# Attention and routed experts on one core: three of four turns of the values moved from the fifth block of a step to the first block of the next one

## The chip, the core and the metric

The kernel runs on one core of a Trainium2 chip. The metric is the device time of one execution in microseconds, taken as the median of several. A core has five engines that run side by side, each through its own queue in order: PE (matrix products; its weight loads, PEld, run beside them), DVE (VectorE), ACT (ScalarE), POOL (GpSimd) and SP (SyncE, which here issues DMAs). They meet through semaphores.

## The reference, cut to what matters

The program computes attention with rotary positions and feeds the result to a layer of routed experts. There are 8 batches of 8 heads, 576 positions, 64 features each.

```python
q_rot, k_rot = (rotate(q), rotate(k))
scores = scale * np.matmul(q_rot, k_rot.transpose(0, 1, 3, 2))
scores = scores - np.max(scores, axis=-1, keepdims=True)
attn = np.exp(scores)
attn = attn / (np.sum(attn, axis=-1, keepdims=True) + 1e-09)
attn_out = np.matmul(attn, v)                    # (8, 8, 576, 64)

x = attn_out.transpose(0, 2, 1, 3).reshape(4608, 512)
y_dense = np.maximum(x @ w1_dense, 0.0) @ w2_dense
logits = x @ w_gate                              # 8 experts
expert_idx = np.argmax(logits, axis=1)           # softmax of logits gives gate_w
y_moe[mask] = gate_w[mask, None] * (np.maximum(x[mask] @ w1[e], 0.0) @ w2[e])   # for each expert e
out = y_dense + y_moe
```

## The kernel before, in words

**Stages.** Attention takes the span from about 29 to 318 us of the profiled execution, the experts' layer the rest. Attention runs over 32 pairs of heads, four pairs to a batch. All of it is issued in program order (a manual schedule), so each engine's queue holds its instructions in the order in which the Python code calls them; no planner moves anything.

**A step and its blocks.** The main loop runs over steps i and, inside a step, over blocks t = 0 to 8. Three pairs are in the works at once. In block t of step i:

- `s1_block(i + 2, t)`, the **scores** of the pair two steps ahead, row-wise: two products on PE (lines 365 and 369, tile `s` of PSUM tag `s1`, two buffers), and DVE takes each row's maximum from them (line 371, `negm`).
- `s2_strip(i, t)`, the **logits** of the present pair, key-wise, with the maximum already folded in: a product on PE (lines 389, 390, 392; PSUM tag `s2`, two buffers), and ACT takes the exponential from it into `pm` (line 409).
- `av_part(i - 1, k)`, the product of the previous pair's exponentials with the values (line 431), from block 1 on; one part of five products in most blocks, two parts in some. After block 8 `av_scale` divides on DVE (lines 442 to 445).

In block 1, `shift_rows(i + 1)` turns the next pair's maxima on PE (line 377, `mps`, tag `s2`), splits them on ACT and DVE (lines 379 and 380, `mT`) and sends them by two DMAs into two rows of `qT` (line 382). The logits of the next step need these rows. After block 8 come the tails, `s2_tails` (lines 389, 390 and 392 again, exponentials on line 416): a use of tag `s2` for the last 64 queries of eight key blocks, and one for the ninth.

**The values.** Each pair's values are loaded in fp32 (`vf`), cast to fp16 on ACT (`cast_v`, line 273) into `v16s`, and turned: `v_turn` (lines 281 and 282) makes five 128 by 128 transposes on PE into a PSUM tile `vps` of tag `s2`, and ACT copies them into `vT`. When all four pairs of a batch are turned, `v_gate` (line 290) multiplies them by the gate's weights at the end of the batch's first step, i = 4b, and `v_part` (lines 298 and 300) puts the result beside the values, so that the attention product also gives the experts' logits. The table `v_steps` says in which step and block a cast and a turn are called; turns of this table come after the block's scores, logits and value products.

**Tag `s2`.** Logits, tails, shifts, turns and gates take the two buffers of this tag by turns. A use can begin when all readers of the use before last are through.

**Other work beside it.** POOL rotates the queries and keys of later pairs (lines 314 to 317) and issues the loads of the experts' weights (line 226); SP issues the transposing DMAs (`qT<-nat`, line 327), the copies of keys (`kx<-qT`, line 355), and the loads. From step 27 on the routing of the first six batches is computed between the blocks, on DVE, POOL, ACT and PE.

Of the kernel before, what the change touches and what calls it, by code (L numbers as in the profile page):

```python
# [25 lines left out]
def kernel(  # L26
# [40 lines left out]
    for i in range(VB):  # L67
        t = const_p.tile([P, HP, 5, 2 * VC], fp16, name=f"v16_{i}")
# [6 lines left out]
    with tc.tile_pool(name="setup", bufs=1) as setup_p:  # L75
# [37 lines left out]
        for b0, b1 in ((0, 5), (5, 9)):  # L113
            n = b1 - b0
# [242 lines left out]
    def s1_block(i, t):  # L357
        qT, kT = (x[0:KM] for x in state["qkT", i])
        if t == 0:
            state["negm", i] = ap.tile([P, 9], f32, tag="negm", bufs=3, name="negm")  # L360
        ps = pp.tile([P, 2, 512], f32, tag="s1", bufs=2, name="s1")
        for c in range(2):
            if t == 4:
                for r0, q0, k0 in ((0, AT, A0), (64, BT, B0)):
                    nc.tensor.matmul(ps[r0:r0 + 64, c, 0:CH], lhsT=qT[:, q0:q0 + 64],  # L365
                                     rhs=kT[:, k0 + c * CH:k0 + (c + 1) * CH], start=True, stop=True)
            else:
                k0 = A0 if t < 4 else B0
                nc.tensor.matmul(ps[:, c, 0:CH], lhsT=qT[:, t * P:(t + 1) * P],  # L369
                                 rhs=kT[:, k0 + c * CH:k0 + (c + 1) * CH], start=True, stop=True)  # L370
        nc.vector.tensor_reduce(state["negm", i][:, t:t + 1], ps[:, :, 0:CH], axis=AX.XY, op=AL.max, negate=True)  # L371
# [299 lines left out]
    def attention():  # L671
        for f in turn_early(0):
            f()
        stage_keys(1, nc.sync)
        for part in range(2):
            stage_load(1, 0, 2, part, (0, HP))
        split_gate()
        for i in range(1, KK):
            pad_keys(i)
        for t in range(9):  # L680
            s1_block(0, t)
        for t in range(9):
            s1_block(1, t)
            if t == 1:
                shift_rows(0)
                for part in range(2):
                    stage_load(1, 2, 4, part, ())
                nc.scalar.copy(ident_h, ident_f)
                nc.scalar.preload_act_table_set("natural_log_exp_and_others")
                cast_v(0, 0)  # L690
            if t == 2:
                early_2 = turn_early(2)
            if 3 <= t < 7:
                early_2[t - 3]()
        cast_v(0, 1)
        for i in range(3, RA):
            stage_rope(i)
        stage_transpose(3)
        gt = gate_steps(0, wg)
        rk, got0 = rank_steps(0, wg, attn_sums)  # L700
        WS = [(i, 5) for i in range(5, 22, HP)] + [(24, 5), (25, 1), (25, 6), (26, 1), (26, 6)]
        assert len(WS) == E + 2
        steps = {(27, 0): gt[0:1], (22, 0): [route_first, route_ranks, route_tokens], (27, 2): gt[1:2], (27, 4): gt[2:3]}
        AVS = (((0, 0), (0, 1), (1, 3), (3, 4), (4, 5), (5, 7), (7, 8), (8, 9), (9, 10)),
               ((0, 0), (0, 1), (1, 3), (3, 4), (4, 5), (5, 6), (6, 7), (7, 8), (8, 10)))
        loads = {}
        for b in range(2, B):
            n = (b - 2) * HP
            for at, f, *x in ((n, stage_load, b, 0, 2, 0, ()), (n + 1, stage_load, b, 0, 2, 1, ()),
                              (n + 1, stage_tails, b, 0), (n + (1 if b in (2, B - 1) else 2), stage_tails, b, 1),  # L710
                              (n + 2, stage_load, b, 2, 4, 0, ()), (n + 3, stage_load, b, 2, 4, 1, ())):
                loads.setdefault(at + (1 if b == 2 else 0), []).append((f, *x))
        V0 = (0, 2), (0, 7), (1, 3), (1, 5)
        v_steps = {}
        for b in range(1, B):
            n = b * HP
            for u, (c, r) in enumerate((((n - 3, 6), (n - 3, 8)), ((n - 2, 3), (n - 2, 5)), ((n - 1, 3), (n - 1, 5)), ((n, 2), (n, 5)))):
                if b == B - 1 and u > 1:
                    c = (n - 1, 1 + 3 * (u - 2))
                if b == 1 and u < 2:  # L720
                    c, r = ((n - 2, 1), (n - 2, 5)) if u == 0 else ((n - 2, 6), (n - 2, 8))
                v_steps.setdefault(c, []).append((cast_v, b, u))
                v_steps.setdefault(r, []).append((v_turn, b, u))
        for i in range(NP + 1):
            for t in range(9):
                if i + 2 < NP:
                    s1_block(i + 2, t)
                if i < NP:
                    s2_strip(i, t)
                if 1 <= i <= NP and t >= 1:  # L730
                    for k in range(*AVS[i % HP == 1][t]):
                        av_part(i - 1, k)
                    if t == 8:
                        av_scale(i - 1)
                if i == 0 and t in (3, 5):
                    cast_v(0, 2 + t // 5)
                if (i, t) in V0:
                    v_turn(0, V0.index((i, t)))
                if i < NP and (i, t) in v_steps:
                    for f, *x in v_steps.pop((i, t)):  # L740
                        f(*x)
                if t == 1 and i + 1 < NP:
                    shift_rows(i + 1)
                if t == 2 and i + RA < NP:
                    stage_rope(i + RA)
                if t == (0 if i > 1 else 2) and i + KA < NP:
                    stage_keys(i + KA, nc.sync)
                if t == 2 and i + LA < NP:
                    stage_transpose(i + LA)
                if t == 2:  # L750
                    for f, *x in loads.pop(i, ()):
                        f(*x)
                if (i, t) in WS:
                    n = WS.index((i, t))
                    load_w(*((w1d, moe_w1_dense), (w2d, moe_w2_dense))[n] if n < 2 else (w1e[:, n - 2], moe_w1[n - 2]))
                if t == 5:

                    if i % HP == 0 and i // HP + 1 < B:
                        stage_v(i // HP + 1)
                    if i % HP == 3 and HP < i < NP - HP or i == NP - 3:  # L760
                        x_store(i // HP - 1)
                    if i == NP - RA:
                        early_cm.__exit__(None, None, None)
                        open_late()
                        wa = late["wa"]
                        pl, mm, fin = plan_steps(0, wa, attn_sums, got0)
                        w2 = [lambda e=e: load_w(late["w2e"][:, e], moe_w2[e]) for e in range(E)]
                        steps[27, 6] = rk[0:1] + [route_parts]
                        steps[27, 5] = w2[0:2]
                        steps[27, 7] = w2[2:5]  # L770
                        steps[28, 0] = rk[1:2] + w2[5:6] + pl[0:1]
                        steps[28, 2] = gt[3:4]
                        steps[28, 3] = rk[2:3] + w2[6:8] + pl[1:2]
                        steps[28, 6] = rk[3:4]
                        steps[29, 0] = pl[2:3]
                        steps[30, 5] = pl[3:4]
                        steps[29, 3] = pl[4:6]
                        steps[29, 8] = rk[4:5]
                        steps[30, 0] = rk[5:6]
                        steps[30, 2] = mm + [fin, lambda: draw(0, 0)]  # L780
                        steps[30, 6] = [lambda: draw(0, 2)]
                if (i, t) == (NP - 2, 4):
                    logit_sum(B - 2)
                for st in steps.pop((i, t), ()):
                    st()
            if i < NP:
                s2_tails(i, 0)
            if i < NP:
                s2_tails(i, 1)
            if i in (0, 1) or i < NP and i % HP == 0:  # L790
                u0, u1 = (2 * i, 2 * i + 2) if i < 2 else (0, HP)
                for u in range(u0, u1, 2):
                    v_gate(u)
                v_part(i // HP, 0, u0, u1)
                steps.setdefault((i + 1, 0), []).append(lambda b=i // HP, u0=u0, u1=u1: v_part(b, 1, u0, u1))
            if i == NP - 1:
                draw(1, 0)
                draw(1, 2)
        assert not steps and not v_steps and not loads
        logit_sum(B - 1)  # L800
        x_store(B - 1)

# [248 lines left out]
```

## Time and profile before

| | |
|---|---|
| median of 3 runs | 466.23 us (463.81 to 466.33) |
| the profiled execution | 465.76 us |
| its span, first to last instruction | 464.0 us |
| mean granted clock of PE | 0.984 |
| busy: PE, DVE, ACT, POOL | 404.8, 320.5, 294.0, 342.3 us |
| transposes of the values (line 281) | 160, busy 14.1 us |
| copies of the turned values (line 282) | 32, busy 22.1 us, 692 ns each |
| exponentials of the logits (line 409, 512 wide) | 280, 598 ns each |
| maxima of the scores (line 371) | 288, 749 ns each |

How to read it: busy times are sums over the span, and a group's mean is the time from an instruction's start to its end; the next one on the same engine can begin a little before that. In the order of time each row gives start, length, engine, line, operation, out<-in, shapes and count, and in brackets the engine's idle time before it with what ended it.

### The profile page before, as it was taken

The page shows a single profiled execution, that of the slowest core. Times are in us where ns is not written, and L with a number is a line of the kernel's source. Part 1 is how long each engine was busy: PE and PEld are TensorE (multiplying, and loading weights), DVE is VectorE, ACT ScalarE, POOL GpSimd, SP SyncE. Part 2 cuts the span into 40 slices and gives each one's busy share as a digit, 9 for nine tenths or more (in the row PEclk, how much of TensorE's full clock was granted, in tenths as well). Part 3 has the DMA queues.
Part 4 walks back from the last instruction along what each step waited for, and adds up shares of the span by engine and source line. Part 5 has one row for each costly group of instructions (what it writes and reads, how often), then busy time and mean ns, then how long its engine had stood idle before and what let it go on. Part 6 is the DMA issues. An engine that isn't in the chain of part 4 may idle for free.

```text
span 464.0 us, 11073 instructions
## 1 busy us (share of the span) xinstructions
PE 404.8 (87%) x4108; PEld 250.0 (54%) x4108; DVE 320.5 (69%) x580; ACT 294.0 (63%) x571; POOL 342.3 (74%) x279
## 2 busy tenths in 40 slices
PE   1788898889999999999998879777999999999992
PEld 0346566666666666666666556554344544444440
DVE  7886799889999899899899899933357221111221
ACT  6588787877887987887887876653443323333320
POOL 1799999989999889999999958834464456652332
PEclk9999999999999999999999998989999999999998
DMA  6886669987867967988959999954988588996452
GB/s 177 227 172 156 119 159 243 143 198 209 178 192 195 179 192 201 167 194 209 202 151 209 157 148 220 217 95 95 207 193 163 135 202 190 199 188 147 97 146 84
DMA packets 134250, 80.65 MB, mean 174 GB/s; under 512 B 93460, under 2 KB 127764, under 8 KB 134196
## 3 DMA queue, kind: packets, MB, share of 16 engines
q1 hardware_dynamic: 119684, 55.93, 54.0%
q0 software_dynamic: 14240, 23.73, 25.2%
q8 instruction: 35, 0.57, 0.5%
q10 hardware_dynamic: 272, 0.26, 0.2%
q14 instruction: 19, 0.16, 0.1%
HBM read 52.05 MB, written 14.42 MB: 143 GB/s over the span
## 4 chain that ended last, share of the span: by engine, by line
PE 62%; DVE 11%; DMA 10%; ACT 9%; issue 3%; SPq 2%; another core or an unknown queue 1%; POOLq 0%; POOL 0%; ACTq 0%; DVEq 0%
PE s L369 10%; PE s L392 9%; PE av L431 9%; PE py L922 7%; PE py L920 7%; PE pe L905 6%; PE pd L896 6%; DVE negm L371 5%; ACT pm L409 5%; DMA qT<-mT 3%; DMA kx<-qT 2%; PE vps L281 2%; PE s L365 2%; PE s L389 2%; DMA vf<-in_v_dram 2%
## 5 line engine op out<-in xcount | busy, mean ns | idle before, releaser
L371 DVE TENSOR_REDUCE negm<-s 128x1 f32<-128x576 f32 x288 | 205.3, 749 | 20.3 <-PE s L369 19.0
L409 ACT ACTIVATE pm<-s 128x512 f16<-128x512 f32 x280 | 161.3, 598 | 42.0 <-PE s L392 36.1
L431 PEld LDWEIGHTS <-pm 128*128 128x128 f16 x1600 | 87.1, 98 | 53.8 <-issue 21.4
L392 PE MATMUL s<-qT,kx 128*128 128x64 bf16 (+1 forms) x504 | 107.0, 285 | 9.8 <-ACT pm L409 4.5
L369 PE MATMUL s<-kx,qT 126*128 126x288 bf16 x512 | 108.0, 294 | 6.3 <-DVE negm L371 4.3
L431 PE MATMUL av<-v,pm 128*128 128x82 f16 x1600 | 100.5, 201 | 1.0 <-DVE v L300 0.7
L314 POOL TENSOR_TENSOR ra<-qk,cosx 128x1152 bf16<-128x1152 f32 x30 | 78.9, 2630 | 20.1 <-DVE nat L317 10.9
L924 DVE COPY y<-py 128x512 f32<-128x512 f32 x37 | 25.2, 690 | 86.0 <-PE py L922 66.9
L925 POOL DMA_INDIRECT out_dram<-y,put_i x37 | 38.1, 1030 | 57.9 <-DVE y L924 49.2
L908 ACT ACTIVATE hn<-pe,gp 128x512 bf16<-128x512 f32 x37 | 25.4, 687 | 75.5 <-PE pe L905 35.0
L317 POOL TENSOR_TENSOR nat<-ra,rb 128x1152 bf16<-128x1152 bf16 x30 | 70.9, 2363 | 2.4
L851 POOL DMA_INDIRECT xg<-xd,take_i x37 | 35.8, 967 | 25.7 <-issue 9.4
L369 PEld LDWEIGHTS <-qT 126*128 126x128 bf16 x512 | 40.2, 99 | 20.9 <-issue 13.1
L905 PE MATMUL pe<-w1e,xs 128*128 x148 | 38.9, 385 | 4.2 <-ACT hn L908 2.5
L392 PEld LDWEIGHTS <-kx 128*128 128x128 bf16 x512 | 35.1, 97 | 13.1 <-issue 5.2
L315 POOL TENSOR_TENSOR rb<-qk,sinx 128x576 bf16<-128x576 f32 x30 | 42.2, 1406 | 0.0
L316 POOL TENSOR_TENSOR rb<-qk,sinx 128x576 bf16<-128x576 f32 x30 | 42.1, 1404 | 0.0
L896 PE MATMUL pd<-xs,w1d 128*128 128x512 bf16 (+1 forms) x160 | 38.6, 369 | 0.2 <-ACT hd L898 0.2
L922 PE MATMUL py<-w2e,he 128*128 x148 | 38.0, 379 | 0.5 <-DMA he<-hn 0.5
L920 PE MATMUL py<-w2d,hd 128*128 128x512 bf16 x148 | 38.0, 379 | 0.0
L898 ACT ACTIVATE hd<-pd 128x512 bf16<-128x512 f32 (+1 forms) x40 | 22.6, 565 | 10.1 <-PE py L922 4.8
L443 DVE TENSOR_TENSOR xn<-av,rz 128x640 bf16<-128x640 f32 x32 | 26.4, 825 | 1.1
(178 smaller groups left out, 428.0 us busy)
## 6 DMA issues: line engine op xcount, KB each, us to landing
vf<-in_v_dram SPq DMA_DIRECT2D x8, 1024.0 KB
qk<-in_q_dram SPq DMA_DIRECT2D x15, 512.0 KB
qk<-in_k_dram SPq DMA_DIRECT2D x15, 512.0 KB
kx<-qT SPq DMA_DIRECT2D x30, 144.0 KB
xd<-xn SPq DMA_DIRECT2D x8, 512.0 KB
w1e<-in_moe_w_dram POOLq DMA_DIRECT2D x8, 512.0 KB
w2e<-in_moe_w_dram POOLq DMA_DIRECT2D x8, 512.0 KB
vf<-in_v_dram SPq DMA_DIRECT2D x16, 64.0 KB
```

The costliest lines, as they stand in the source:

```text
L314: eng.tensor_tensor(a, x, cx, AL.mult)
L315: eng.tensor_tensor(s[:, :, :, 0:half], x[:, :, :, half:D], sx[:, :, :, 0:half], AL.mult)
L317: eng.tensor_tensor(nat.rearrange("p c w d -> p w c d"), a, s, AL.add)
L369: nc.tensor.matmul(ps[:, c, 0:CH], lhsT=qT[:, t * P:(t + 1) * P], rhs=kT[:, k0 + c * CH:k0 + (c + 1) * CH], start=True, stop=True)
L371: nc.vector.tensor_reduce(state["negm", i][:, t:t + 1], ps[:, :, 0:CH], axis=AX.XY, op=AL.max, negate=True)
L392: nc.tensor.matmul(out_ap, lhsT=kT[:, s * P:(s + 1) * P], rhs=qT[:, qa if s < 4 else qb], start=True, stop=True)
L409: nc.scalar.activation(state["pm", i][:, ORDER.index(s), 0:MAIN], ps, AF.Exp, scale=float(scale))
L431: nc.tensor.matmul(state["av"][:, h, x * VC:(x + 1) * VC], lhsT=state["pm", i][:, 4 * h + n if n < 4 else 8, q0:q0 + P], rhs=v16s[b % VB][ ...
L896: nc.tensor.matmul(ps[:, 0:n], lhsT=w1d[:, dt, ft * P:(ft + 1) * P], rhs=xs[:, 0:n, dt, :], start=(dt == 0), stop=(dt == DT - 1))
L905: nc.tensor.matmul(ps, lhsT=xs[:, u, dt, :], rhs=w[:, 0, dt, :], start=(dt == 0), stop=(dt == DT - 1))
L920: nc.tensor.matmul(py, lhsT=hd[:, ft, u], rhs=w2d[:, ft, :], start=(ft == 0), stop=False)
L922: nc.tensor.matmul(py, lhsT=he[:, ft], rhs=w[:, 0, ft, :], start=False, stop=(ft == FT - 1))
```

## The change

In the table of casts and turns the turns of the first three pairs of a batch get another place: the first block of the step after the one in which they stood (for the pair whose turn stood in block 8, likewise the next step's first block). An entry with block 0 goes into a second table, `v_first`, which the loop calls between the scores and the logits of the block. The fourth turn of each batch keeps its place in block 5 of step 4b; for batch 1 the first two turns keep theirs too, and the turns of batch 0 are not in the table. The casts stay.

```diff
-        v_steps = {}
+        v_steps, v_first = {}, {}
         for b in range(1, B):
             n = b * HP
-            for u, (c, r) in enumerate((((n - 3, 6), (n - 3, 8)), ((n - 2, 3), (n - 2, 5)), ((n - 1, 3), (n - 1, 5)), ((n, 2), (n, 5)))):
+            for u, (c, r) in enumerate((((n - 3, 6), (n - 2, 0)), ((n - 2, 3), (n - 1, 0)), ((n - 1, 3), (n, 0)), ((n, 2), (n, 5)))):
                 if b == B - 1 and u > 1:
                     c = (n - 1, 1 + 3 * (u - 2))
                 if b == 1 and u < 2:
                     c, r = ((n - 2, 1), (n - 2, 5)) if u == 0 else ((n - 2, 6), (n - 2, 8))
                 v_steps.setdefault(c, []).append((cast_v, b, u))
-                v_steps.setdefault(r, []).append((v_turn, b, u))
+                (v_steps if r[1] else v_first).setdefault(r, []).append((v_turn, b, u))
         for i in range(NP + 1):
             for t in range(9):
                 if i + 2 < NP:
                     s1_block(i + 2, t)
+                for f, *x in v_first.pop((i, t), ()):
+                    f(*x)
                 if i < NP:
                     s2_strip(i, t)
```

More of the change, by code (lines that the diff above doesn't have):

```diff
@@ L798, in attention @@
                 draw(1, 2)
-        assert not steps and not v_steps and not loads
+        assert not steps and not v_steps and not v_first and not loads
         logit_sum(B - 1)
```

## The prediction

> **What bounds the kernel now.** I read three views in turn: the chain that ended last, the busy time of each engine step by step, and the order of time inside one step.
>
> ```profile
> PE 62%; DVE 11%; DMA 10%; ACT 9%; issue 3%; SPq 2%; another core or an unknown queue 1%; POOLq 0%; POOL 0%; ACTq 0%; DVEq 0%
> PE s L369 10%; PE s L392 9%; PE av L431 9%; PE py L922 7%; PE py L920 7%; PE pe L905 6%; PE pd L896 6%; DVE negm L371 5%; ACT pm L409 5%; DMA qT<-mT 3%; DMA kx<-qT 2%; PE vps L281 2%; PE s L365 2%; PE s L389 2%; DMA vf<-in_v_dram 2%
> ```
>
> The turns themselves (vps, L281) are on the chain: 2% of 464.0 us. The chain is PE's; the next view says how tightly. Its columns are stretch, length, then busy us (and instructions) of PE, PEld, DVE, ACT, POOL, then clock, DMA share, GB/s; the stretches are steps 10, 11, 12, 13, each from its first exponential to the next step's.
>
> ```profile
> 120.66:128.64 7.98, 7.68 (x98) 5.44 (x97) 7.38 (x13) 6.97 (x15) 7.33 (x5) 1.00 0.89 152
> 128.64:136.64 8.00, 7.71 (x98) 5.43 (x97) 7.54 (x14) 6.96 (x14) 7.84 (x5) 1.00 0.56 134
> 136.64:145.86 9.22, 8.65 (x138) 6.48 (x137) 8.80 (x16) 7.41 (x16) 9.06 (x5) 1.00 0.90 251
> 145.86:154.92 9.06, 7.98 (x98) 5.41 (x97) 8.26 (x15) 7.25 (x15) 8.96 (x6) 1.00 0.84 208
> ```
>
> These four steps are one batch, 34.3 us. I call them by i mod 4: **two** (step 10), **three** (11), **zero** (12), **one** (13). PE and DVE are both nearly full, so what matters is who waits inside a step. The order of time from block 5 of step 11 to block 3 of step 12:
>
> ```profile
> 132.38 0.53 PE L431 MATMUL av<-v,pm 128*128 128x82 f16 x10
> ...
> 132.81 0.44 PE L281 MATMUL vps<-ident_h,v 128*128 128x128 f16 x5
> ...
> 133.09 0.41 PE L369 MATMUL s<-kx,qT 126*128 126x288 bf16 x2
> ...
> 133.29 0.69 ACT L282 COPY vT<-vps 128x640 f16<-128x640 f16 x1
> ...
> 133.54 2.10 DVE L371 TENSOR_REDUCE negm<-s 128x1 f32<-128x576 f32 x3 [0.42 <-PE s L369]
> ...
> 133.88 1.81 ACT L409 ACTIVATE pm<-s 128x512 f16<-128x512 f32 x3
> ...
> 135.59 0.71 ACT L416 ACTIVATE pm<-s 128x512 f16<-128x512 f32 x2
> 135.74 0.19 PE L389 MATMUL s<-qT,kx 128*64 128x64 bf16 x1 [0.26 <-ACT pm L409]
> ...
> 135.90 0.42 PE L369 MATMUL s<-kx,qT 126*128 126x288 bf16 x2
> ...
> 136.23 0.38 PE L392 MATMUL s<-qT,kx 128*128 128x512 bf16 x1
> ...
> 136.45 0.41 PE L369 MATMUL s<-kx,qT 126*128 126x288 bf16 x2
> ...
> 136.64 1.08 ACT L409 ACTIVATE pm<-s 128x512 f16<-128x512 f32 x2 [0.35 <-PE s L392]
> 136.69 0.38 PE L392 MATMUL s<-qT,kx 128*128 128x512 bf16 x1
> ...
> 137.29 0.28 PE L377 MATMUL mps<-ident_f,negm 128*9 128x128 f32 x1
> ...
> 137.57 0.41 PE L369 MATMUL s<-kx,qT 126*128 126x288 bf16 x2
> ...
> 137.81 0.38 PE L392 MATMUL s<-qT,kx 128*128 128x512 bf16 x1
> ...
> 138.40 0.41 PE L369 MATMUL s<-kx,qT 126*128 126x288 bf16 x2
> ```
>
> Read it in two halves. From block 3 to block 6 PE runs without a gap and DVE ends up waiting for it (0.42 us at 133.54): PE is the bound there, and the turn lies in it, 132.81 to 133.09. From the tails of step 11 to block 3 of step 12 the bound is the ring of two PSUM buffers that logits, tails, turns, shifts and gates share: each use waits until ACT has emptied the use before last. PE waits 0.26 us for an exponential at 135.74, and the logits at 136.23 start 0.04 us after the tails' exponential ends (135.59, and 0.60 for that width, a row of which stands below).
>
> **The change part by part.** Of the 28 turns in the loop's list, 19 move: one into the head of step 4, and three per batch into the heads of steps 6-8, 10-12, 14-16, 18-20, 22-24 and 26-28. Each issues what it issued before: five transposes, which hold PE 0.28 us, and one copy, which holds ACT 0.59 us (133.29 to 133.88). No DMA moves, and the casts of the values stay where they are, well ahead. Nothing changes in amount, only in whose way it stands.
>
> *What leaving block 5 gives.* The scores of block 6 start 0.28 us sooner, and DVE has 0.42 us of idle time there to take that up: -0.28 us in steps two and three. In step zero nothing leaves; its fourth turn stays.
>
> *What arriving at the head costs.* I keep block 6 of step 11 at 133.09 and carry the rows on with the turn at the head of step 12. The turn takes the buffer that the logits had, so its transposes start when those did, 136.19 (the copy that left block 5 gives back 0.04), and the copy runs from 136.67 to 137.36. ACT can take the first exponential 0.59 after the copy's start, at 137.26 instead of 136.64. The second logits need the buffer of the turn: 137.40 instead of 136.69. Behind them wait the shift (first exponential done at 137.86, so 137.90 instead of 137.29), the scores of block 2, and the second exponential (137.82 to 138.42), for which the logits of block 2 wait: 138.46 instead of 137.81. PE is in order, so block 3 begins at 139.05 instead of 138.40: **+0.65 us**. DVE has finished its own part by then (its reduction of block 2 comes 0.5 us later than before and its 0.42 us of idle time covers the difference), and the stretch from block 3 on is PE's, so nothing gives it back. Step three: +0.65 - 0.28 = +0.37. Step zero: +0.65.
>
> *Step two* differs, since its turn comes from block 8 of step one, where it already stood in the ring. Block 8's exponential on ACT, block 8's scores on PE, and what PE did after them:
>
> ```profile
> 118.31 0.60 ACT L409 ACTIVATE pm<-s 128x512 f16<-128x512 f32 x1
> ```
>
> ```profile
> 117.35 0.41 PE L369 MATMUL s<-kx,qT 126*128 126x288 bf16 x2
> ```
>
> ```profile
> 118.48 0.44 PE L281 MATMUL vps<-ident_h,v 128*128 128x128 f16 x5
> 118.96 0.39 PE L392 MATMUL s<-qT,kx 128*128 128x64 bf16 x8
> 119.75 0.19 PE L389 MATMUL s<-qT,kx 128*64 128x64 bf16 x1 [0.40 <-ACT vT L282]
> ...
> 121.31 0.28 PE L377 MATMUL mps<-ident_f,negm 128*9 128x128 f32 x1
> 121.43 0.41 PE L369 MATMUL s<-kx,qT 126*128 126x288 bf16 x2
> ...
> 122.39 0.41 PE L369 MATMUL s<-kx,qT 126*128 126x288 bf16 x2
> ```
>
> Without it the tails take 118.48, the short tail 118.95 (when 118.31 + 0.60 is over), the scores 119.10; the tails' exponential ends at 119.51, so the turn starts at 119.55, its copy 120.03 to 120.72, second logits 120.77, second exponential to 121.79, block 3 at 122.42 against 122.39. Moving it within the head gives nothing (+0.04); leaving block 5 gives -0.28: -0.23 together. **A batch: -0.23 + 0.37 + 0.65 = +0.79 us**; batches 3 to 6 make +3.16.
>
> *The ends of the loop* have waits of their own that swallow part of this.
>
> ```profile
> 94.00 0.38 PE L392 MATMUL s<-qT,kx 128*128 128x512 bf16 x1 [1.04 <-DMA qT<-mT]
> ```
>
> ```profile
> 258.50 0.38 PE L392 MATMUL s<-qT,kx 128*128 128x512 bf16 x1 [0.76 <-DMA qT<-mT]
> 266.93 0.41 PE L369 MATMUL s<-kx,qT 126*128 126x288 bf16 x2 [0.73 <-DMA kx<-qT]
> ```
>
> ```profile
> 278.43 0.41 PE L369 MATMUL s<-kx,qT 126*128 126x288 bf16 x2 [1.69 <-DVE negm L371]
> ```
>
> At 94.00 (head of step 7) PE waits 1.04 us for a transfer; all that steps 3 to 6 gain or lose (-0.28 + 0.65 - 0.23 = +0.14) goes into it, and so does the turn at that head. Step 7 then keeps -0.28 and step 8 +0.65: +0.37. At 258.50 and 266.93 transfers are late behind expert weights that POOL issues at its own pace:
>
> ```profile
> 197.62 2.61 POOL L314 TENSOR_TENSOR ra<-qk,cosx 128x1152 bf16<-128x1152 f32 x1 [1.38 <-DMA qk<-in_k_dram]
> ```
>
> ```profile
> POOL ra L314 <- DMA qk<-in_k_dram: 1.4, 1, 1.4
> ```
>
> The second row is the whole answer on POOL's waits from 198 to 268 us: it is the wait of the first row and no other. So POOL falls back by what the loop had lost at 197.62, 0.37 and two batches of 0.79 or about 2 us, while PE falls back 3.5; some 1.5 us of late transfers can be absorbed. I take the 0.76 whole, and let the 0.73 cover all but 0.2 of the turn at step 27's head. At step 28's head PE idles 1.69 us for DVE: that turn is free, and the one that left step 27 was covered by the routing on DVE. Batch 7: -0.23 - 0.76 + 0.2 = -0.79.
>
> **Sum:** 0.37 + 3.16 - 0.79 = +2.7 us on the profiled execution's own 465.76 (span 464.0 and 1.8 around it): 468.5. The median of the runs, 466.23, lies 0.5 above that execution; I give 468.8, between 468.5 and 469.0. Bounds of the unseen part: if no wait absorbs anything, batches 1 to 7 make 0.37 + 5 x 0.79 + 0.42 = +4.7; if the head costs half (ACT and PE each hide some), 0.33 less at ten heads (two each in batches 3 to 6, steps 8 and 27), -0.6.
>
> [...]
>
> **Rivals.** *The head hides the turn.* ACT idles 0.35 us at 136.64 and PE 0.26 at 135.74; if the transposes and copy fill those, every departure is profit: block 8 to block 3 takes 5.04 us into step 10 (117.35, 1.13 before the row at 118.48, to 122.39) and 3.97 into step 12 (134.43, below, to 138.40), of which 0.18 is five more values products, so 0.9 per batch at step two and 0.28 at two and three: -1.45 x 5 batches, -7 us, 459. It decides by whether the first exponential still starts where it did; against it, the copy needs the tails' exponential out of the ring first, so it cannot begin before 136.67, when ACT's idle time is over.
>
> ```profile
> 134.43 0.41 PE L369 MATMUL s<-kx,qT 126*128 126x288 bf16 x2
> ```
>
> *Nothing absorbs*, and shifts issued 0.6 us later in the step make transfers late: +4.7 and more, 471 to 473. For it: the two waits at 258 and 267 exist; against: those two are tied to POOL. *The clock.* The stretch with the longest idle time shows the price:
>
> ```profile
> 28.80:94.40 65.60, 56.87 (x719) 39.30 (x719) 55.60 (x93) 53.19 (x105) 63.63 (x34) 1.00 0.77 156
> ...
> 276.50:289.20 12.70, 10.45 (x141) 7.65 (x140) 11.57 (x28) 7.23 (x15) 9.96 (x21) 0.87 1.20 216
> ```
>
> 0.13 of 12.7 us is 1.7 us; at 19 heads, +31, 497. [...] Against it, the first row: many waits of up to 1 us at clock 1.00. *No change at all*, if DVE were the true bound: against it, its 0.42 us of idle time. That the edit is not done is no rival: the queue's order is written out by hand, and each copy now stands between the short tail's exponential and the step's first one.
>
> **How the numbers follow.** The forecast as told, +1 to +4.5: 0.62. Nothing absorbs: 0.18. Head hides the turn: 0.10. No change: 0.08. Clock: 0.02. A change of 1% (4.7 us) is about what a measurement of this kernel can tell from none. Faster than that: 0.08 (most of the hiding case). Slower: 0.20 (nothing absorbs, the clock). Within: 0.72. The range takes in no change with the runs' own spread (463.81 to 466.33) and the unabsorbed case up to 472.5.
>
> **What would show it.** Steps three and zero longer by 0.37 and 0.65, step two shorter by 0.2; the waits at 258 and 267 gone or small; at the heads PE's second logits waiting for vT; DVE's 0.42 us in step two mostly gone. I am wrong if step zero keeps its 9.2 us.

## The result

| | before | after |
|---|---|---|
| median of 20 runs each, taken together | 463.15 us (460.69 to 468.52) | 466.76 us (463.77 to 471.7) |
| the profiled execution | 465.76 us | 468.41 us |
| its span | 464.0 us | 466.7 us |
| mean granted clock of PE | 0.984 | 0.982 |

After divided by before is **1.0071 [1.0046, 1.0095]**: 0.71% slower, or 3.3 us of 463.15 (2.1 to 4.4). That is a real loss and a small one. The forecast change was +2.7 us, and the two profiled spans differ by 2.7; the comparison of the terms, below, shows that the second agreement is luck. The forecast of the time itself, 468.8, lies 2.0 us above 466.76, because it started from the median of the first 3 runs of before, 466.23, and 20 runs gave 463.15. Medians here and below are of all runs; the ratios leave disturbed runs out.

The page of after, its span and its chain:

```profile
span 466.7 us, 11073 instructions
...
PE 53%; DVE 12%; DMA 12%; ACT 11%; issue 7%; POOL 3%; SPq 1%; POOLq 0%; ACTq 0%; DVEq 0%
PE s L369 9%; PE s L392 8%; PE av L431 8%; PE py L924 6%; PE py L922 5%; DVE negm L371 5%; ACT pm L409 5%; PE pd L898 4%; PE pe L907 4%; DMA qT<-mT 4%; ACT vT L282 3%; PE vps L281 2%; PE s L365 2%; PE s L389 2%; DMA vf<-in_v_dram 2%
```

A line is new in this list: the copy `ACT vT L282`, 3%. Before, the transposes of the turns (PE L281) were in it with 2%, and the copy behind them was not among its fifteen entries. PE's share falls from 62% to 53%, but the change explains little of that: seven of the nine points are the four rows of the experts' layer (`py` twice, `pe`, `pd`: 26% before, 19% here), which the edit does not touch.

The batch of steps 10 to 13 of after, from each step's first exponential to the next one's, with the columns of the prediction's view (length, busy us and instructions of PE, PEld, DVE, ACT, POOL, clock, DMA share, GB/s):

```profile
122.12:130.44 8.32, 7.71 (x96) 5.38 (x96) 7.44 (x13) 7.08 (x16) 5.98 (x5) 1.00 0.70 136
130.44:138.75 8.31, 7.71 (x96) 5.38 (x96) 7.77 (x14) 7.07 (x15) 8.15 (x5) 1.00 0.59 161
138.75:148.01 9.26, 8.54 (x136) 6.45 (x136) 8.41 (x15) 7.50 (x17) 9.10 (x5) 1.00 0.68 207
148.01:157.09 9.08, 8.10 (x98) 5.39 (x97) 8.81 (x16) 7.24 (x16) 8.98 (x7) 1.00 0.88 225
```

They take 34.97 us, against 34.26 before: **+0.71 a batch**, forecast +0.79. PE's busy time is nearly what it was; the steps are longer by waiting. These windows cut a step within its head, since the first exponential itself moved.

By this view the prediction's own signs fail in two steps of three: step two is longer by 0.34 instead of shorter by 0.2, step three is longer by 0.31, and step zero takes 9.26, so it keeps the 9.2 us that were to show the prediction wrong. The sign was ill chosen; the mechanism held. The turn delays the first exponential, with which a window begins, so most of what a head loses is counted to the step before it. Cut at the scores of block 6, behind which no head reaches, the stretches that end in steps two, three, zero and one take 8.78, 8.32, 8.59 and 9.27 us, against 9.03, 8.01, 7.94 and 9.28 before: -0.25, +0.31, +0.65 and 0.0, where -0.23, +0.37, +0.65 and nothing were forecast. So from here on I measure by the scores of block 8, of the next step's block 3 and of block 6.

Steps 11 and 12 of after in order of time (PE, ACT, and one row of DVE):

```profile
131.98 5.15 DVE L371 TENSOR_REDUCE negm<-s 128x1 f32<-128x576 f32 x7
132.24 0.41 PE L369 MATMUL s<-kx,qT 126*128 126x288 bf16 x2
...
134.59 0.41 PE L369 MATMUL s<-kx,qT 126*128 126x288 bf16 x2
...
135.89 0.41 PE L369 MATMUL s<-kx,qT 126*128 126x288 bf16 x2
...
137.20 0.19 PE L389 MATMUL s<-qT,kx 128*64 128x64 bf16 x1 [0.26 <-ACT pm L409]
...
137.69 0.44 PE L281 MATMUL vps<-ident_h,v 128*128 128x128 f16 x5
...
138.16 0.69 ACT L282 COPY vT<-vps 128x640 f16<-128x640 f16 x1 [0.41 <-PE vps L281]
...
138.75 1.16 ACT L409 ACTIVATE pm<-s 128x512 f16<-128x512 f32 x2
138.91 0.38 PE L392 MATMUL s<-qT,kx 128*128 128x512 bf16 x1 [0.32 <-ACT vT L282]
139.41 0.28 PE L377 MATMUL mps<-ident_f,negm 128*9 128x128 f32 x1
...
139.97 0.38 PE L392 MATMUL s<-qT,kx 128*128 128x512 bf16 x1
...
140.55 0.41 PE L369 MATMUL s<-kx,qT 126*128 126x288 bf16 x2
```

The four rows of L369 are block 3, block 6 and block 8 of step 11, and block 3 of step 12. The head went as it was foretold. Carried to these times (block 6 starts here at 134.59, and in the prediction at 133.09, 1.50 earlier), the prediction has the transposes at 137.69, the copy at 138.17, the first exponential at 138.76, the second logits at 138.90, the shift at 139.40, the third logits at 139.96 and block 3 at 140.55. From block 6 to block 3 is 5.96 us, against 5.31 before: +0.65. From block 8 it is 4.66 against 3.97, because block 8 itself comes 0.04 sooner. PE's second logits wait 0.32 for `vT`, as the prediction said they would. PE's waits by line, from 100 to 200 us of after, show it as a rule (sum in us, times, longest):

```profile
PE s L392 <- ACT vT L282: 2.7, 8, 0.4
```

In step 11, block 3 to block 6 takes 2.35 us (2.36 in the other steps of its kind). Before, it ran from the next row to 133.09, 2.70 us:

```profile
130.39 0.41 PE L369 MATMUL s<-kx,qT 126*128 126x288 bf16 x2
```

So the departure gave 0.34 to 0.35, not 0.28, and DVE took it: its row at 131.98 in after is one unbroken run of seven reductions, where before it idled 0.42 us ahead of block 6.

**The ends of the loop.** The wait at step 7's head and the three late waits of after, on PE:

```profile
93.79 0.38 PE L392 MATMUL s<-qT,kx 128*128 128x512 bf16 x1 [0.24 <-DMA qT<-mT]
...
263.46 0.38 PE L392 MATMUL s<-qT,kx 128*128 128x512 bf16 x1 [0.29 <-DMA qT<-mT]
...
270.63 0.19 PE L389 MATMUL s<-qT,kx 128*64 128x64 bf16 x1 [0.26 <-DMA kx<-qT]
...
272.94 0.38 PE L392 MATMUL s<-qT,kx 128*128 128x512 bf16 x1 [1.39 <-DMA qT<-mT]
```

At step 7's head the wait of 1.04 shrank to 0.24. The wait of 0.76 at step 26's head shrank to 0.29, and from block 8 to block 3 that step takes 5.12 us, as step 10 does, with no late transfer. The 0.73 for `kx` is gone too: the 0.26 put down to it stands at the short tail, which waits 0.26 in other steps as well. But a wait of 1.39 for the shifts' transfer is new at step 27's head. Step 26 thus gained 1.12 and step 27 lost 1.07.

**The clock.** Two steps of after grew by more than the change explains: step 9 by 1.30 us and step 17 by 1.51. Windows around step 9's head in after; the last number but two is the granted clock:

```profile
108.90:112.31 3.41, 2.51 (x60) 2.09 (x57) 3.34 (x7) 2.21 (x5) 3.33 (x2) 1.00 0.96 307
112.31:115.73 3.42, 3.35 (x23) 2.14 (x23) 2.11 (x5) 1.45 (x4) 3.42 (x3) 0.50 0.78 213
```

For one stretch of 3.41 us PE's granted clock was 0.50, and it issued 23 matmuls. The same stretch of time in the second profile of before, taken later and told of below, has 42:

```profile
112.31:115.73 3.42, 3.36 (x42) 2.19 (x42) 3.19 (x6) 2.38 (x5) 3.42 (x3) 1.00 0.71 192
```

The first profile of before has its half-speed stretches late (one starts at 278.76), after's stand at 112.31 and 183.99 and then at 334.18 and 460.47.

### The profile page after: what moved, and what is told of

It is laid out like the page before. It is cut to its first block, busy times and chain, and to the rows that moved or that the text cites. A ratio compares the mean times of both kernels' runs of the same rounds, so it can differ in the third digit from the quotient of the medians.

```text
span 466.7 us, 11073 instructions
## 1 busy us (share of the span) xinstructions
PE 404.7 (87%) x4108; PEld 249.5 (53%) x4108; DVE 323.3 (69%) x580; ACT 297.0 (64%) x571; POOL 342.2 (73%) x279
## 4 chain that ended last, share of the span: by engine, by line
PE 53%; DVE 12%; DMA 12%; ACT 11%; issue 7%; POOL 3%; SPq 1%; POOLq 0%; ACTq 0%; DVEq 0%
PE s L369 9%; PE s L392 8%; PE av L431 8%; PE py L924 6%; PE py L922 5%; DVE negm L371 5%; ACT pm L409 5%; PE pd L898 4%; PE pe L907 4%; DMA qT<-mT 4%; ACT vT L282 3%; PE vps L281 2%; PE s L365 2%; PE s L389 2%; DMA vf<-in_v_dram 2%
## 5 line engine op out<-in xcount | busy, mean ns | idle before, releaser
L369 PE MATMUL s<-kx,qT 126*128 126x288 bf16 x512 | 108.9, 296 | 6.7 <-DVE negm L371 5.0
L369 PEld LDWEIGHTS <-qT 126*128 126x128 bf16 x512 | 40.5, 100 | 18.2 <-issue 11.8
L282 ACT COPY vT<-vps 128x640 f16<-128x640 f16 x32 | 22.1, 692 | 8.7 <-PE vps L281 8.2
```

## The experiments

Times in a row below are starts of scores; "8 to 3" is from block 8 of one step to block 3 of the next, "3 to 6" within a step. Three numbers of before are compared throughout: into step two 5.04, into three and zero 3.97, and 3 to 6 of 2.70 in two and three. Numbers of a place are those of steps 8 to 18, which repeat from batch to batch; where a late transfer or a half-speed stretch lies in a step it is said. Before was timed anew with each group of experiments, and its time was another each time (463.15, 468.11, 469.25), so a kernel is compared with the before taken beside it alone.

### The first turn alone

```diff
-(((n - 3, 6), (n - 2, 0)), ((n - 2, 3), (n - 1, 0)), ((n - 1, 3), (n, 0)), ((n, 2), (n, 5)))   # after
+(((n - 3, 6), (n - 2, 0)), ((n - 2, 3), (n - 2, 5)), ((n - 1, 3), (n - 1, 5)), ((n, 2), (n, 5)))
```

> Only the first turn of batches 2 to 7 is moved (from block 8 of step one to the head of step two); the second and third stay in block 5. Ring theory (a turn at a head delays the next logits by its copy on ACT): block 8 to block 3 into step two 5.12 us against 5.04 before, blocks 3 to 6 of step two 2.70 as before, steps three and zero as before (3.97 and 2.70, 3.97 and 2.63); six batches at +0.05 to +0.1, so +0.5 us, a ratio of 1.000 to 1.002. Rival (the head is a good place and only steps three and zero lose): into step two 4.2 to 4.6, six times -0.5 to -0.9, a ratio of 0.988 to 0.994.

Measured: 467.55 us against 468.11, ratio 0.9981 [0.9948, 1.0013]. Into step ten:

```profile
119.75 0.41 PE L369 MATMUL s<-kx,qT 126*128 126x288 bf16 x2
...
121.95 0.44 PE L281 MATMUL vps<-ident_h,v 128*128 128x128 f16 x5
...
124.87 0.41 PE L369 MATMUL s<-kx,qT 126*128 126x288 bf16 x2
```

That is 5.12, 0.09 above before, and from step 10 to step 24 no other place moves (step 9 has a half-speed stretch; steps 7, 26, 27 and 29 differ by their waits for transfers and by the routing). A turn taken from block 8 and put behind the next step's first scores stays in the same queue for the same two buffers. The rival, that this move by itself gains 0.5 to 0.9, is out.

### The moved turns left out

```diff
-                (v_steps if r[1] else v_first).setdefault(r, []).append((v_turn, b, u))
+                if r[1]:
+                    v_steps.setdefault(r, []).append((v_turn, b, u))
```

> The 19 moved turns are left out altogether (transposes and copies), so the gate reads old turned values, the routing is another one and only the attention steps may be read. Ring theory: block 8 to block 3 is 3.97 into steps three and zero and 4.15 into step two (0.18 for five more value products in block 8); blocks 3 to 6 are 2.36 in steps two and three, as with the turns moved, since PE is the bound there. Rival (DVE is the bound of the step): blocks 3 to 6 stay at 2.5 or more and the heads win nothing, since DVE's reductions, division and scaling fill the step. Second rival (the head hides most of a turn): into step two 4.6 or more.

In this kernel and the next the tile `vT` is also allocated once, and not anew for each batch. Measured: 463.37 us in one run, beside 468.11 of before. Block 8 of step 11 and block 3 of step 12:

```profile
131.67 0.41 PE L369 MATMUL s<-kx,qT 126*128 126x288 bf16 x2
...
135.67 0.41 PE L369 MATMUL s<-kx,qT 126*128 126x288 bf16 x2
```

8 to 3 is 4.00 into three and zero, 4.34 into two (0.19 above what was expected; why was not found), and 3 to 6 is 2.36. The differences give the price of one turn by its place: **0.34 us in block 5** (2.70 - 2.36), 0.70 in block 8 (5.04 - 4.34), **0.66 at the head of three and zero** (4.66 - 4.00), 0.78 at the head of two (5.12 - 4.34). Had DVE been the bound, as one rival had it, a head without its turn would not have fallen back to 4.00.

Two heads of this kernel are longer, with no turn in them: 5.08 into step 19 and 5.16 into step 23. The second has the row below; what holds the first, 0.96 us ahead of the scores of block 0, was not found.

```profile
226.70 0.38 PE L392 MATMUL s<-qT,kx 128*128 128x512 bf16 x1 [1.15 <-DMA qT<-mT]
```

So a transfer that was early enough before is waited for when the steps get shorter, and some of what this kernel gains on a batch is lost in such waits.

### The transposes without the copies

```diff
-        nc.scalar.copy(state["vT"][:, u], ps)
+        if copy:
+            nc.scalar.copy(state["vT"][:, u], ps)
```

The copies of the nineteen turns at heads are left out; their transposes stay.

> The 19 moved turns make their five transposes at the head, into the same shared PSUM tag, but the copies by ACT are left out; the gate reads old turned values, so only the attention steps may be read. Ring theory: without the copy the second logits wait for nothing; block 8 to block 3 into steps three and zero 4.1 to 4.25, so 0.4 to 0.55 of the 0.69 that the move cost belong to the copy. Rival (the transposes on PE carry the cost, ahead of the logits): 4.5 or more.

Measured: 464.02 us in one run, beside 468.11 of before. Block 8 of step 11 and block 3 of step 12 (this kernel's line numbers are one higher):

```profile
132.94 0.41 PE L370 MATMUL s<-kx,qT 126*128 126x288 bf16 x2
...
137.14 0.41 PE L370 MATMUL s<-kx,qT 126*128 126x288 bf16 x2
```

4.20, which lies 0.2 above the head without a turn and 0.45 below the head with one. Into two it is 4.62, 0.28 and 0.50. So at a head two thirds of the price is the copy, which holds its buffer and ACT's time, and one third the transposes. In block 5 the whole price is 0.34, about the transposes' own time on PE, which is the bound there; that the copy costs nothing in block 5 is read from this, and no run leaves it out there alone. Late transfers lengthen two heads here too (4.65 into step 19, 4.80 into 23).

### The turn behind the first logits

```diff
-                for f, *x in v_first.pop((i, t), ()):
-                    f(*x)
                 if i < NP:
                     s2_strip(i, t)
+                for f, *x in v_first.pop((i, t), ()):
+                    f(*x)
```

> The change with one pair of lines swapped: the turn comes behind the first logits of the block instead of ahead of them, so ACT takes the first exponential before the copy. Ring theory: the third use of the head (the shift) now waits for the copy and the second logits wait for the first exponential, so block 8 to block 3 into steps three and zero is 4.45 to 4.6 (3.97 before, 4.66 with the change), and blocks 3 to 6 stay at 2.36 in step three. Rival (it is the late first exponential alone that delays the step): 4.0 to 4.15. Second rival (nothing depends on the order within the block): 4.66.

Measured: 471.51 us in one run, beside 469.25 of before. Block 8 of step 11 and block 3 of step 12:

```profile
135.66 0.41 PE L369 MATMUL s<-kx,qT 126*128 126x288 bf16 x2
...
140.19 0.41 PE L369 MATMUL s<-kx,qT 126*128 126x288 bf16 x2
```

4.53 instead of 4.66 into zero, 4.93 instead of 5.12 into two: letting the first exponential go ahead of the copy gives back 0.13 to 0.19 and no more, since the ring's next user, the shift, now waits for the copy. Its weight load in step 12 shows it:

```profile
139.10 0.09 PEld L377 LDWEIGHTS mps<-ident_f,negm 128*9 128x9 f32 x1 [0.16 <-ACT vT L282]
```

(Step 19, at 5.05, waits 0.43 for a transfer as well.) A batch is at +0.63 over before, against +0.71. Of the 0.63, 0.37 comes from a place that the edit doesn't touch: the head of step one, block 8 to block 3, takes 6.13 from 5.76. The next experiment shows more of it.

### The first turn in block 2

```diff
-(((n - 3, 6), (n - 3, 8)), ((n - 2, 3), (n - 2, 5)), ...   # before
+(((n - 3, 6), (n - 2, 2)), ((n - 2, 3), (n - 2, 5)), ...
```

> The kernel before with one entry changed: the first turn of batches 2 to 7 stands in block 2 of step two instead of block 8 of step one. Ring theory (a turn costs 0.7 to 0.9 at a step's end or head, where ACT's copies and exponentials follow one another, and its time on PE, 0.28 to 0.5, in the middle): block 8 to block 3 into step two 4.4 to 4.65 against 5.04, six times -0.4 to -0.6, -2.4 to -3.6 us, a ratio of 0.992 to 0.995. Rival (a turn costs the same wherever it stands in the ring): 4.85 to 5.05, a ratio of 0.998 to 1.002.

Measured: 468.69 us against 468.11, ratio 0.9968 [0.9928, 1.0008]: no difference shown. Block 8 of step nine, the turn, and block 3 of step ten:

```profile
118.39 0.41 PE L369 MATMUL s<-kx,qT 126*128 126x288 bf16 x2
...
122.73 0.44 PE L281 MATMUL vps<-ident_h,v 128*128 128x128 f16 x5
123.00 0.41 PE L369 MATMUL s<-kx,qT 126*128 126x288 bf16 x2
```

Into two it is 4.61 instead of 5.04, as hoped, though 3 to 6 of that step becomes 2.83 (+0.13). But in steps 9, 13 and 17 the head of step one takes 6.13 instead of 5.76 (6.95 in step 21, which has a half-speed stretch). The shift of step 9 in this kernel:

```profile
113.97 0.28 PE L377 MATMUL mps<-ident_f,negm 128*9 128x128 f32 x1 [0.28 <-ACT pm L409]
```

and in before, with the instructions ahead of it:

```profile
111.58 0.60 ACT L409 ACTIVATE pm<-s 128x512 f16<-128x512 f32 x1
112.03 0.58 DVE L300 TENSOR_TENSOR v<-vw,v 128x320 f16<-128x320 f32 x1
112.24 0.38 PE L392 MATMUL s<-qT,kx 128*128 128x512 bf16 x1 [0.45 <-ACT pm L409]
...
112.65 0.60 ACT L409 ACTIVATE pm<-s 128x512 f16<-128x512 f32 x1 [0.46 <-PE s L392]
...
112.85 0.27 PE L377 MATMUL mps<-ident_f,negm 128*9 128x128 f32 x1
```

In this place the uses of the tag do not take the two buffers by turns, as the description of the kernel has it. The second logits, at 112.24, begin while DVE still reads the gate's tile (112.03 to 112.61), and they wait for the exponential of the first logits: they follow these in the same buffer. The shift of before starts 0.24 us behind the last read of the gate's tile and before the second exponential ends (113.25), so it has the gate's buffer; the shift of this kernel waits for the second exponential, so by this wait it has the other one. -0.43 + 0.13 + 0.37 = +0.07 a batch: the gain was given back three steps later, by an allocation. Before has this 6.13 too, in steps 5 and 25. What decides which of the two buffers a use gets was not found. In the two profiles of before and the two of after it is the same each time, which suggests that it is settled when the kernel is built.

### The first turn in block 7 of the step in which it is cast

```diff
-(((n - 3, 6), (n - 3, 8)), ...   # before
+(((n - 3, 6), (n - 3, 7)), ...
```

> The kernel before with the first turn of batches 2 to 7 one block earlier, in block 7 of step one, right behind its cast. Ring theory: the copy still lies in ACT's closed row of exponentials at the end of the step, so little is won: from block 6 of step one to block 3 of step two 6.1 to 6.35 us against 6.34 before. Rival (only the last block is dear, since there the short tail waits for the copy): 5.6 to 5.9, six times -0.5 and more. If the shift of step one waits for the same buffer as before, block 8 to block 3 into step one stays at 5.76.

Measured: 468.27 us in one run, beside 469.25 of before. The turn, block 8 of step nine, and block 3 of step ten:

```profile
118.68 0.45 PE L281 MATMUL vps<-ident_h,v 128*128 128x128 f16 x5 [0.47 <-ACT v L273]
118.97 0.41 PE L369 MATMUL s<-kx,qT 126*128 126x288 bf16 x2
...
123.18 0.41 PE L369 MATMUL s<-kx,qT 126*128 126x288 bf16 x2
```

Into two 4.21, a gain of 0.83, but block 6 to block 8 of step nine is longer by 0.92, 2.22 instead of 1.30: together 6.43, where 6.1 to 6.35 were expected, 0.09 lost instead of a small gain. The first row says where half of the 0.92 comes from: the cast, in block 6, is not done, and PE stands 0.47 us with the scores of block 8 queued behind the turn. The turn then holds PE for 0.29 until these scores; the rest was not taken apart. The head of step one stays at 5.76, as was expected if its shift keeps its buffer.

### Both kernels again

> The kernel before once more, for the clock alone. [...] Rival (each kernel has its own stretches, and the change brought those at steps 9 and 17): the same stretches as in the first profile, near 278.8, 309.5 and 323.1 us.

> The changed kernel once more, for the clock alone. Theory: half-speed stretches at other steps than 9 and 17; the batches without one still last 0.71 us longer than before's. Rival: stretches again in steps 9 and 17 (112.3 and 184.0 us).

Measured: 468.68 and 474.07 us, one run each. From step 1 to step 25 the times of before repeat to 0.02 us, but for the heads of steps 6 and 7 (5.62 and 5.06, then 6.08 and 4.60: the same sum), where transfers are waited for; and a batch of after without slow clock (steps 14 to 17) again costs 0.71 more. What does not repeat is the clock. In the second profile of after, the head of step 9, then that of step 13:

```profile
112.31:115.73 3.42, 2.91 (x37) 1.85 (x34) 3.21 (x6) 2.43 (x6) 3.42 (x3) 1.00 0.89 260
...
148.01:151.42 3.41, 3.41 (x24) 2.15 (x24) 2.10 (x5) 1.42 (x3) 3.33 (x3) 0.51 0.90 251
```

Steps 9 and 17 run at full speed now, and 13 and 21 are hit (clock 0.51 from 148.01 to 151.42, 0.50 from 219.60 to 223.00), by 1.3 and 1.5 us. In the second profile of before two half-speed stretches follow each other, from 268.19 to 275.02, and step 27's head takes 3.1 us more than in the first, with a late transfer in it. The first of the two:

```profile
268.20:271.60 3.40, 2.48 (x13) 1.52 (x14) 0.79 (x2) 1.54 (x3) 0.59 (x1) 0.50 1.00 159
```

So the rival that each kernel has its own slow stretches is out: they move between executions of one kernel. Nor does the wait of 1.39 us at step 27's head repeat. In the second profile of after PE waits there for the turn alone:

```profile
273.25 0.38 PE L392 MATMUL s<-qT,kx 128*128 128x512 bf16 x1 [0.32 <-ACT vT L282]
```

and in the second of before for the transfer, longer still:

```profile
269.12 0.59 PE L392 MATMUL s<-qT,kx 128*128 128x512 bf16 x1 [2.03 <-DMA qT<-mT]
```

The wait for that landing varies from one execution to the next by more than the change moves it.

## Why the prediction was right, and where its terms were off

Set against the first profiles:

| term | forecast, us | measured, us |
|---|---|---|
| leaving block 5 (steps two and three) | -0.28 | -0.34, and block 8 0.04 sooner, which the head's term counts |
| head of three and zero, from block 6 | +0.65 | +0.65 (+0.69 from block 8) |
| head of two | +0.04 | +0.09 |
| a batch | +0.79 | +0.71 |
| batches 1 and 2 | +0.37 | -0.24 |
| batches 3 to 6, without the clock | +3.16 | +2.84 |
| batch 7 | -0.79 | -0.05 |
| sum | +2.7 | +2.55 |

- **The head.** For steps three and zero right to 0.01 us, instruction by instruction; for step two 0.05 short. What carried it was to follow each use of the ring in order and to ask, for each, which reader of the use before last is through last. The experiment without copies confirms the split: 0.45 by ACT's copy, 0.2 by the transposes.
- **Leaving block 5.** Right in kind, mis-sized by 0.06. The prediction took the time from the first transpose to the next scores. Measured, the stretch is 0.34 shorter; something ahead of the first transpose goes with it too. Whether that is the turn's own first weight load was not tried.
- **Batches 1 and 2.** "All that steps 3 to 6 gain or lose goes into" the 1.04 us at step 7's head: the wait did absorb that turn, but its end is not fixed. It ended at 94.00 in both profiles of before and at 93.79 in after (the first row under "The ends of the loop"). That is 0.21 earlier, in an execution whose loop began 0.39 later: 0.60 earlier against the loop, which makes up the miss of 0.61. The transfer was issued later than in before (87.18 and 86.55), so it took less time, and why was not found. An absorbing wait that itself moves is no anchor.
- **Batch 7.** The wait of 0.76 at step 26 went as forecast (-1.12 for -0.99). The step that failed is "let the 0.73 cover all but 0.2 of the turn at step 27's head": in its place came a new wait of 1.39 us, +1.07. The other profiles show it absent in one and 2.03 in another, so this term has no settled value, only a spread of some 2 us. The prediction gave it 0.2 without bounds.
- **The misses cancel within 0.2 us** (-0.61 - 0.32 + 0.74). The sum is better than its terms, and that is luck: the two largest misses belong to transfers and have opposite signs.
- **The clock.** The rival was written as +31 us at 19 heads, with a chance of 0.02, and in that form it did not come. A smaller form that the prediction did not list did: 2.8 us in steps 9 and 17 of after. With 0.39 us that the two executions differ already in step 1, the trace stands at +5.7 us in step 28. Between 308 and 336 us, where before has slow stretches at 309.48 and 323.13 and after one at 334.18, the lead of before over the same instructions of after falls from 5.7 below zero and returns to 2.8, and over the span it is 2.7; that the clock alone does this was not shown. So the equal 2.7 of forecast and spans is luck. The ratio of the runs, +2.1 to +4.4, is the better witness. The clock-free sum of 2.55 lies in it, but the ratio does not tell how much of the loss is the clock's.
- **The other rivals.** That the head hides the turn: no; leaving nineteen turns out gives 1.40 a batch against before (-0.70 - 0.38 + 0.03 - 0.38 + 0.03), about the 1.45 that the rival counted on, so its price was right and its condition was not met. That nothing absorbs: not in this form; step 26's wait did absorb. That DVE is the bound: no, by the head that fell back to 4.00.

**What stays open.** Whether the change makes slow stretches more frequent. Steps 1 to 24 of before had none in its two profiles, those of after two, and three with one in step 1. My reason to ask is an estimate: a batch of before is 34.26 us, close to ten times 3.41 (34.13), one of after 34.97, a quarter of 3.41 more, so that its heads move against the starts of such stretches from batch to batch. That this has an effect was not shown. The counts are of two executions each, and no run tells them apart from chance; against the estimate, two kernels whose batch is only 0.1 longer than before's had such stretches too, the one with the first turn alone moved at 113.55 and the one with that turn in block 2 at 76.43 and 216.37. The clocks of the 20 runs of before are not on record, so the runs cannot settle it.

## What to carry to other kernels

A short piece of work on two engines has no one price: the same turn cost 0.34 us where PE was the bound and its buffer's other users were not waiting, and 0.66 to 0.78 at the head of a step, where a shared ring of two buffers made everyone wait for its copy. So an idle slot on an engine is no free place; ask which buffer the work takes and who needs that buffer next, and look for a gain given back by the allocation steps later. And a wait for a transfer may be counted on to swallow work only if its end stays where it is: one such wait had no fixed length from one execution to the next, and another ended at 94.00 in both executions of before and still moved with the change.

## What the hardware showed that was not expected

**The clock fell in stretches of one length.** Inside attention the stretches with a granted clock of 0.50 last 3.41 us, or twice that where two follow each other (268.19 to 275.02 in the second profile of before), and within one execution they start whole multiples of 3.413 us apart: after's 112.31 and 183.99 are 71.68 us apart, 21 times that, before's 278.76 and 309.48 are 30.72 apart, nine times. Those of after cost 1.30 us in step 9 and 1.51 in step 17. Among the 20 runs of after the three with a mean clock of 0.973 or less took 466.9 to 471.7 us, the four with 0.988 or more 464.44 to 466.18; the order is loose, for the fastest of all, 463.77, had 0.980. Ahead of the stretch shown PE was busy 2.51 of 3.41 us (108.90 to 112.31, clock 1.00, with the gate's 40 narrow products in it), and ahead of the one at 183.99 it was busy 2.47 (180.58 to 183.99, clock 1.00). No rule follows from this: in after PE was busy 1.87 of 3.42 us from 310.29 on, and the next 3.41 us had clock 1.00. What tells such places apart was not found.

**Which of two buffers a use gets can cost 0.37 us a batch**, as the shift in the experiment with block 2 shows (5.76 or 6.13 for the same head), in kernels whose order of work in that head is the same.
